# K and V pages of two neighbouring heads in one transfer of 256 rows, in half of each layer of a two-layer decode kernel

## The chip, the cores and the metric

One Trainium2 chip; the kernel runs on one of its cores. The core has a matrix engine (PE, with its weight loads shown apart as PEld), a vector engine (DVE), a scalar engine (ACT), a general engine (POOL) and a sync engine (SP) whose queue (SPq) issues the transfers. Sixteen DMA engines move the data from the chip's main memory (HBM) into the on-chip memory (SBUF, 128 partitions).

The metric is the device time of one launch in microseconds (us), the median of several runs. Beside it stands one profiled execution, whose span runs from its first to its last instruction.

## The reference

One token passes twice through the same attention block and the same gated feed-forward block (the layers are called 0 and 1 here; both read the same weights and the same caches):

```
x = x + A(layernorm(x));  x = x + B(layernorm(x));  x = x + A(layernorm(x));  x = x + B(layernorm(x))

A: q = x @ wq                                   # 640 -> 32 heads of 192
   scores = q . k[last 4096 rows] / sqrt(192)   # per head, 4096 x 192 bf16 = 1.5 MiB
   o = softmax(scores) @ v[last 4096 rows]      # per head, another 1.5 MiB
   return o @ wo                                # 6144 -> 640
B: return (silu(x @ w1) * (x @ w3)) @ w2        # 640 -> 1536 -> 640
```

The last 4096 of 32768 rows are used of each head's K and V. All of it is bf16, with one row of activations, so nearly all bytes are read for a single product. Since both layers use the same caches, a page of K that stays in SBUF need not be read a second time.

## The kernel before, in words

**Slots.** SBUF holds an `arena` of 16 slots (`NSLOT`), each 128 partitions x 6144 bf16 (12288 bytes per partition, 1536 KB), one page each. A page is one head's K or V window, a fifth of `wq`, or a piece of `wo`, `w1`, `w3`, `w2`. Slot s begins at element `s * PGW` of each partition's row of the one tile `arena`.

**Order of the loads.** Before anything is recorded, a list `loads` is made (L163 to L198), for each layer: five pages of `wq`; then for i = 0 to 37 the V page of place i-6 (`LEAD` is 6) and the K page of place i, as far as these exist; then `wo`, `w1`, `w3`, `w2`. A place g (0 to 31) is turned into a head by `head(layer, g)`: layer 0 takes the heads in blocks of eight as 24-31, 16-23, 8-15, 0-7, layer 1 as 8-15, 0-7, 16-23, 24-31.

**Retained pages.** The K pages of the 14 heads in `RETAIN` (0 to 8, 11, 14, 18, 21, 24) are kept from layer 0 for layer 1; their slots come free only in layer 1. One of them, head 24 (`STASH`), is copied by DVE out of its slot and back later (`stash`, L214); in layer 1 it takes a slot without a transfer. So the number of slots that circulate falls in the second half of layer 0, down to 3, and rises again in the first half of layer 1.

**Slots and transfers.** `refill` (L200) takes the next entry of `loads` as long as a slot is free, and records one `dma_start` on SP's queue into that slot (L210). `free` is first in, first out. `done(key)` (L225) puts a page's slot back on `free` when the last instruction that reads it has been recorded, and calls `refill`. All instructions are kept in the order in which they are recorded (`pin`), SP's included. A framework puts in the semaphore waits: a transfer waits for the last readers of its slot, a reader waits for the transfers that write what it reads, and each transfer also waits for the transfer eight before it, because the transfers share eight semaphores in turn. To tell which accesses touch each other, the framework compares their regions of the tile.

**Work on a page.** `attention` (L494) runs steps i = 0 to 37. In step i it first uses the V page of place i-6 (`v_page`, 16 matmuls, group `o_ps`), then the K page of place i (`k_page`): DVE turns the page in place in two halves (L300, `k_turn`), and PE multiplies it (12 matmuls, group `s_ps`). A retained K page was already turned in layer 0. After each fourth K page come the turn of the next K page, a softmax (`softmax_head`, L321 on), and a step later the placing of its result (`softmax_place`, L343). A block of four heads is closed by `combine` (L372). After step 37 follow `wo_proj` (group `y_ps`), a layernorm and `ffn` (groups `g_ps`, `u_ps`, and in layer 1 `f_ps`).

All matmuls have one line, L80, the helper that records them; they are told apart by their groups.

Of the kernel before, what the change touches and what calls it, by code (L numbers as in the profile page):

```python
# [15 lines left out]
P = 128  # L16
# [9 lines left out]
PGW = 6144  # L26
# [5 lines left out]
RETAIN = (0, 1, 2, 3, 4, 5, 6, 7, 8, 11, 14, 18, 21, 24)  # L32
# [4 lines left out]
MW = 2 * HB  # L37
PW = MW * (HB - 1) + 32
KSPLIT = 2


def _ap(t, p0, npart, off, dims):
    ps = t.ap[0][0]
    return bass.AP(t.tensor, t.offset + p0 * ps + off, [[ps, npart]] + [list(d) for d in dims])
# [3 lines left out]
def kernel(  # L48
# [13 lines left out]
    nc = tc.nc  # L62
    SK = A_k_cache.shape[2]
    S0 = SK - WIN
# [10 lines left out]
    def pin(ins):  # L75
        tc.keep_in_program_order(ins)
        return ins
# [60 lines left out]
    arena = arn.tile([P, NSLOT * PGW], BF16, name="arena")  # L138
# [3 lines left out]
    free = list(range(NSLOT))  # L142
    home = {}
    turned = set()
    loads = []

    wq_v = A_wq.rearrange("(p c) n -> c p n", c=NCH)
    wo_v = A_wo.rearrange("(b p e) n -> b p (e n)", b=H // HG, p=P, e=12)
    w1_v = B_w1.rearrange("(p c) n -> p (c n)", c=NCH)
    w3_v = B_w3.rearrange("(p c) n -> p (c n)", c=NCH)  # L150
    w2_v = B_w2.rearrange("(p f) n -> p (f n)", f=12)
# [3 lines left out]
    def head(layer, g):  # L155
        return HG * ORDER[layer][g // HG] + g % HG

    def wo_order(layer):
        last = ORDER[1][3]
        kept = [12 * ORDER[layer].index(last) + e for e in (9, 10, 11)]  # L160
        return [ci for ci in range(48) if ci not in kept] + kept

    for layer in range(2):  # L163
        for c in range(NCH):
            loads.append((("q", layer, c), [(0, PGW, wq_v[c])]))
        for i in range(H + LEAD):
            for kind, g, cache in (("v", i - LEAD, A_v_cache), ("k", i, A_k_cache)):
                if not 0 <= g < H:
                    continue
                h = head(layer, g)  # L170
                if kind == "k" and layer == 1 and h in RETAIN:
                    if h == STASH:
                        loads.append((("k", 1, h), []))
                    continue
                loads.append(((kind, layer, h),
                              [(0, PGW, cache[0, h, S0:SK, :].rearrange("(p t) d -> p (t d)", p=P))]))
        for w in range(6):
            parts = []
            for at, ci in enumerate(wo_order(layer)[9 * w:9 * w + 9]):
                blk, e = ORDER[layer][ci // 12], ci % 12  # L180
                if parts and parts[-1][2] == blk and parts[-1][3] + parts[-1][1] == e:
                    parts[-1][1] += 1
                else:
                    parts.append([at, 1, blk, e])
            parts = [(640 * at, 640 * n, wo_v[blk][:, 640 * e:640 * (e + n)]) for at, n, blk, e in parts]
            if w < 5:
                loads.append((("o", layer, w), parts))
            elif layer == 0:
                assert len(parts) == 1 and parts[0][1] == 1920
                loads.append((None, [(wo5[:], parts[0][2])]))  # L190
        loads.append((("fa", layer), [(0, PGW, w1_v[:, 0:PGW])]))
        loads.append((("fb", layer), [(0, PGW, w3_v[:, 0:PGW])]))
        loads.append((("fc", layer), [(0, 1536, w1_v[:, PGW:]), (1536, 1536, w3_v[:, PGW:]),
                                      (3072, 2560, w2_v[:, 0:2560])]))
        fd = [(0, 3200)] if layer == 0 else [(0, 1280), (1280, 1280), (2560, 640)]
        loads.append((("fd", layer), [(o, n, w2_v[:, 2560 + o:2560 + o + n]) for o, n in fd]))
        if layer == 0:
            loads.append((None, [(keep[:], w2_v[:, 5760:7680])]))  # L198

    def refill():  # L200
        while loads and (free or loads[0][0] is None):
            key, parts = loads.pop(0)
            if key is None:
                for dst, src in parts:
                    pin(nc.sync.dma_start(out=dst, in_=src))
                continue
            s = free.pop(0)
            home[key] = s
            for off, n, src in parts:
                pin(nc.sync.dma_start(out=arena[:, s * PGW + off:s * PGW + off + n], in_=src))  # L210
            if not parts:
                stash(arena[:, s * PGW:s * PGW + PGW], False)

    def stash(x, save):  # L214
        xu, pu, ru = x.bitcast(U32), pss[:].bitcast(U32), rest[:].bitcast(U32)
        at = 0
        for t, lo, n in [(pu, 512 * k, 512) for k in range(5)] + [(pu, MB + MN, 512 - MN), (ru, 0, MN)]:
            a, p = xu[:, at:at + n], t[:, lo:lo + n]
            pin(nc.vector.tensor_copy(out=p if save else a, in_=a if save else p))
            at += n  # L220

    def page(key):
        return arena[:, home[key] * PGW:home[key] * PGW + PGW]

    def done(key):  # L225
        free.append(home.pop(key))
        refill()
# [64 lines left out]
    def k_turn(layer, g):  # L292
# [4 lines left out]
        x = page(key)  # L297
        w = PGW // KSPLIT
        for sp in range(KSPLIT):
            pin(nc.vector.transpose(x[:, w * sp:w * (sp + 1)].bitcast(U32), x[:, w * sp:w * (sp + 1)].bitcast(U32)))  # L300
# [193 lines left out]
    def attention(layer):  # L494
# [30 lines left out]
        wo_proj(layer)  # L525

    refill()
    for layer in range(2):
        attention(layer)
# [32 lines left out]
```

## Time and profile before

| what | value |
|---|---|
| median of 3 runs | 528.83 us (528.5 to 529.74) |
| the profiled execution | 528.32 us |
| its span | 526.6 us |
| mean granted TensorE clock | 0.716 |
| PE busy | 275.0 us (52%), 2403 matmuls |
| DVE busy | 256.4 us (49%), 393 instructions |
| ACT busy | 62.5 us (12%) |
| SP's transfers | 221.59 MB, 99.3% of the 16 DMA engines' span |
| K and V pages loaded | 50 K and 64 V, median 29.2 us from issue to landing |

The busy rows are shares of the whole span. The row of the transfers is the time that packets took, as a share of the span of all 16 DMA engines together. The chain of work that ended last is followed back from the last instruction to what released it; its shares by engine add up to the span.

### The profile page before, as it was taken

The numbers are of one execution on the slowest core, as the hardware profiler recorded it, in microseconds if no ns is written. First come the engines' busy times: TensorE is split into PE (matmuls) and PEld (weight loads), VectorE is DVE, ScalarE is ACT, GpSimd is POOL, SyncE is SP. The second block draws the span as 40 slices with busy tenths as digits, with TensorE's granted clock in tenths as the row PEclk, the third lists the DMA queues.
The fourth block names the chain that finished last, engine by engine and source line by source line (L and its number), as shares of the span: only waits on it lengthen the run. The fifth ranks groups of instructions, "written<-read, shape, count | busy, mean of one in ns | idle before, by whom it ended". The sixth has DMA issues, their size and how long they took to land.

```text
span 526.6 us, 5978 instructions
## 1 busy us (share of the span) xinstructions
PE 275.0 (52%) x2403; PEld 112.6 (21%) x2403; DVE 256.4 (49%) x393; ACT 62.5 (12%) x192; POOL 16.2 (3%) x74
## 2 busy tenths in 40 slices
PE   2344644472655644455545555687254756345455
PEld 1111211131222221122112112233022322112113
DVE  1199676556657475654002139531475645753001
ACT  1002020110102020112001002022111120202000
POOL 4000000000000000000000000000000000001000
PEclk9997968666756776586556558988677886686557
DMA  8999999999999999999999999999999999999995
GB/s 349 429 430 433 426 428 427 433 432 427 427 428 432 432 426 429 428 432 423 419 431 422 427 428 427 420 431 427 428 428 431 429 428 429 429 431 428 424 432 242
DMA packets 22355, 221.97 MB, mean 421 GB/s; under 512 B 2616, under 2 KB 2744, under 8 KB 5176
## 3 DMA queue, kind: packets, MB, share of 16 engines
q1 hardware_dynamic: 22184, 221.59, 99.3%
q8 instruction: 19, 0.31, 0.2%
q14 instruction: 8, 0.07, 0.0%
q10 hardware_dynamic: 144, 0.00, 0.0%
HBM read 221.58 MB, written 0.00 MB: 421 GB/s over the span
## 4 chain that ended last, share of the span: by engine, by line
DMA 85%; PE 7%; DVE 5%; issue 1%; ACT 1%; SPq 1%; DVEq 0%; ACTq 0%
DMA arena<-in_A_k_cache_dram 51%; DMA arena<-in_A_v_cache_dram 16%; DMA arena<-in_A_wo_dram 9%; DMA arena<-in_B_w_dram 6%; DMA arena<-in_A_wq_dram 3%; DVE arena L300 3%; PE s_ps L80 3%; PE o_ps L80 2%; PE y_ps L80 1%; SPq L210 1%; PE q_ps L80 1%; PE u_ps L80 0%; PE pss L80 0%; ACT w L337 0%; DVE t L322 0%
## 5 line engine op out<-in xcount | busy, mean ns | idle before, releaser
L80 PE MATMUL s_ps<-arena,wst 128*32 128x512 bf16 x768 | 153.7, 512 | 171.3 <-DVE arena L300 84.5
L300 DVE STREAM_TRANSPOSE arena<-arena 128x1536 uint32<-128x1536 uint32 x100 | 171.2, 1754 | 75.0 <-DMA arena<-in_A_k_cache_dram 74.6
L80 PE MATMUL o_ps<-arena,ptm 128*8 128x384 bf16 (+1 forms) x1024 | 113.5, 421 | 12.9 <-DMA arena<-in_A_v_cache_dram 12.9
L80 PEld LDWEIGHTS <-wst 128*32 128x32 bf16 x768 | 53.1, 115 | 256.2 <-issue 227.1
L80 PEld LDWEIGHTS <-ptm 128*8 128x8 bf16 (+1 forms) x1024 | 40.0, 99 | 49.9 <-issue 40.3
L332 ACT ACTIVATE tb<-m 32x16 f32<-32x16 f32 x16 | 3.4, 214 | 280.4 <-DVE m L329 280.4
L350 ACT COPY ptm<-w 32x64 bf16<-32x64 bf16 x80 | 23.6, 295 | 42.5 <-PE o_ps L80 39.3
L80 PE MATMUL y_ps<-arena,otd 128*1 128x320 bf16 x180 | 16.9, 459 | 15.1 <-DMA arena<-in_A_wo_dram 15.1
L80 PE MATMUL q_ps<-arena,xs 128*32 128x512 bf16 x120 | 14.5, 624 | 17.3 <-DMA arena<-in_A_wq_dram 14.7
L383 DVE SCALAR_TENSOR_TENSOR w<-pss,rl,mask 64x192 bf16<-64x192 f32 x16 | 6.7, 417 | 32.2 <-PE pss L80 32.2
L282 POOL COPY wst<-qt_sb 32x24 bf16<-32x24 bf16 x30 | 8.4, 281 | 432.7 <-PE s_ps L80 313.8
L340 DVE STREAM_TRANSPOSE w<-w 64x512 bf16<-64x512 bf16 x16 | 11.3, 705 | 14.4 <-ACT w L337 14.4
L248 DVE CAST w<-y_ps 128x320 bf16<-128x320 f32 x3 | 1.5, 490 | 34.4 <-PE y_ps L80 34.4
L322 DVE TENSOR_REDUCE t<-s_ps 64x1 f32<-64x512 f32 x16 | 10.6, 663 | 12.2 <-PE s_ps L80 12.1
L274 DVE CAST qt_sb<-pss 32x192 bf16<-32x192 f32 x2 | 0.7, 346 | 31.2 <-PE pss L80 31.2
L350 DVE COPY ptm<-w 32x64 bf16<-32x64 bf16 x48 | 9.9, 207 | 10.8 <-PE o_ps L80 9.6
L80 PEld LDWEIGHTS <-xs 128*32 128x32 bf16 x200 | 7.2, 119 | 35.7 <-issue 26.1
L355 DVE RECIPROCAL rl<-pss 64x1 f32<-64x1 f32 x16 | 2.6, 166 | 22.2 <-PE pss L80 22.2
L80 PEld LDWEIGHTS <-otd 128*1 128x1 bf16 x192 | 6.4, 103 | 25.8 <-issue 21.7
L337 ACT ACTIVATE w<-s_ps,nbt 64x512 bf16<-64x512 f32 x16 | 10.9, 682 | 5.6 <-DVE nbt L334 5.6
L376 ACT CAST w<-o_ps 128x384 bf16<-128x384 f32 x16 | 7.7, 479 | 33.0 <-PE o_ps L80 23.7
L80 PE MATMUL pss<-w,sel 128*64 128x192 bf16 x32 | 6.3, 286 | 9.5 <-ACT w L376 6.4
(82 smaller groups left out, 111.8 us busy)
## 6 DMA issues: line engine op xcount, KB each, us to landing
arena<-in_A_v_cache_dram SPq DMA_DIRECT2D x64, 1536.0 KB, 29.2
arena<-in_A_k_cache_dram SPq DMA_DIRECT2D x50, 1536.0 KB, 29.2
arena<-in_A_wq_dram SPq DMA_DIRECT2D x10, 1536.0 KB, 9.3
arena<-in_A_wo_dram SPq DMA_DIRECT2D x6, 1440.0 KB, 15.3
arena<-in_B_w_dram SPq DMA_DIRECT2D x4, 1536.0 KB, 11.1
arena<-in_A_wo_dram SPq DMA_DIRECT2D x4, 960.0 KB, 16.8
arena<-in_A_wo_dram SPq DMA_DIRECT2D x4, 480.0 KB, 21.8
arena<-in_B_w_dram SPq DMA_DIRECT2D x4, 384.0 KB, 14.6
```

The source lines that it names most:

```text
L80: return pin(nc.tensor.matmul(*a, **k))
L210: pin(nc.sync.dma_start(out=arena[:, s * PGW + off:s * PGW + off + n], in_=src))
L282: pin((engs[a].copy if engs[a] is nc.scalar else engs[a].tensor_copy)(out=dst, in_=src))
L300: pin(nc.vector.transpose(x[:, w * sp:w * (sp + 1)].bitcast(U32), x[:, w * sp:w * (sp + 1)].bitcast(U32)))
L322: pin(nc.vector.reduce_max(out=t0[:, 0:1], in_=s_ps[0:64, :], axis=AX.X))
L332: pin(nc.scalar.mul(out=tb[32:64, :].rearrange("p (a z) -> p a z", a=4)[:, :, 0:HB], in_=mb, mul=-SCALE))
L337: pin(nc.scalar.activation(out=e[:], in_=s_ps[0:64, :], func=ACTF.Exp, bias=nbt[:, 0:1], scale=SCALE, accum_out=l[:]))
L340: pin(nc.vector.transpose(et[:], e[:]))
L350: pin((eng.copy if eng is nc.scalar else eng.tensor_copy)(out=dst, in_=src))
L355: pin(nc.vector.reciprocal(out=rl[half], in_=rl_ps[half]))
L376: pin(nc.scalar.copy(out=o_sb[:, 0:384], in_=o_ps[:, 0:384]))
L383: pin(nc.vector.scalar_tensor_tensor(out=om, in0=ot_ps[half], scalar=rl[half], in1=mask[half].unsqueeze(2).broadcast_to([64, 16, 12]), op0 ...
```

## The change

In the first 16 places of layer 0 and the last 16 places of layer 1 (`PAIRS`), the pages of places g and g+1 (g even) are loaded by one transfer, where both are to be loaded: the entry of `loads` then names two keys, stands at the place of the first, and its source is `cache[0, h:h+2, ...]` seen as 128 rows x 2 heads x 6144. In layer 1 a K pair with a retained head in it (18/19, 20/21, 24/25) is left as it was. That makes 16 pairs in layer 0 and 13 in layer 1 (8 of V, 5 of K).

`refill` now waits, in recording, until as many slots are free as the entry has keys, takes the first ones of `free`, sorts them, and records one `dma_start` whose destination is one access pattern over both slots: 128 partitions x 2 (with a step of the distance between the two slots) x 6144. Pages are used and given back one by one as before.

```diff
+PAIRS = (range(0, 16), range(16, 32))
...
                 h = head(layer, g)
+                if g in PAIRS[layer] and (kind == "v" or layer == 0 or not {h - g % 2, h - g % 2 + 1} & set(RETAIN)):
+                    if g % 2 == 0:
+                        loads.append(([(kind, layer, h), (kind, layer, h + 1)],
+                                      [(0, PGW, cache[0, h:h + 2, S0:SK, :].rearrange("h (p t) d -> p h (t d)", p=P))]))
+                    continue
...
     def refill():
-        while loads and (free or loads[0][0] is None):
-            key, parts = loads.pop(0)
-            if key is None:
+        while loads:
+            keys, parts = loads[0]
+            if keys is None:
                 for dst, src in parts:
                     pin(nc.sync.dma_start(out=dst, in_=src))
+                loads.pop(0)
                 continue
-            s = free.pop(0)
-            home[key] = s
-            for off, n, src in parts:
-                pin(nc.sync.dma_start(out=arena[:, s * PGW + off:s * PGW + off + n], in_=src))
+            n = len(keys)
+            if len(free) < n:
+                return
+            at = sorted(free.pop(0) for _ in range(n))
+            home.update(zip(keys, at))
+            loads.pop(0)
+            s = at[0]
+            for off, w, src in parts:
+                dst = arena[:, s * PGW + off:s * PGW + off + w]
+                if n > 1:
+                    dst = _ap(arena[:], 0, P, s * PGW, [[(at[1] - s) * PGW, 2], [1, PGW]])
+                pin(nc.sync.dma_start(out=dst, in_=src))
             if not parts:
                 stash(arena[:, s * PGW:s * PGW + PGW], False)
```

All other entries of `loads` are wrapped in a list of one key and load as before.

More of the change, by code (lines that the diff above doesn't have):

```diff
@@ L164 @@
         for c in range(NCH):
-            loads.append((("q", layer, c), [(0, PGW, wq_v[c])]))
+            loads.append(([("q", layer, c)], [(0, PGW, wq_v[c])]))
         for i in range(H + LEAD):
@@ L170 @@
                 h = head(layer, g)
+                if g in PAIRS[layer] and (kind == "v" or layer == 0 or not {h - g % 2, h - g % 2 + 1} & set(RETAIN)):
[3 more added lines that the diff above has]
+                    continue
                 if kind == "k" and layer == 1 and h in RETAIN:
                     if h == STASH:
-                        loads.append((("k", 1, h), []))
+                        loads.append(([("k", 1, h)], []))
                     continue
-                loads.append(((kind, layer, h),
+                loads.append(([(kind, layer, h)],
                               [(0, PGW, cache[0, h, S0:SK, :].rearrange("(p t) d -> p (t d)", p=P))]))
@@ L186 @@
             if w < 5:
-                loads.append((("o", layer, w), parts))
+                loads.append(([("o", layer, w)], parts))
             elif layer == 0:
@@ L190 @@
                 loads.append((None, [(wo5[:], parts[0][2])]))
-        loads.append((("fa", layer), [(0, PGW, w1_v[:, 0:PGW])]))
-        loads.append((("fb", layer), [(0, PGW, w3_v[:, 0:PGW])]))
-        loads.append((("fc", layer), [(0, 1536, w1_v[:, PGW:]), (1536, 1536, w3_v[:, PGW:]),
+        loads.append(([("fa", layer)], [(0, PGW, w1_v[:, 0:PGW])]))
+        loads.append(([("fb", layer)], [(0, PGW, w3_v[:, 0:PGW])]))
+        loads.append(([("fc", layer)], [(0, 1536, w1_v[:, PGW:]), (1536, 1536, w3_v[:, PGW:]),
                                       (3072, 2560, w2_v[:, 0:2560])]))
         fd = [(0, 3200)] if layer == 0 else [(0, 1280), (1280, 1280), (2560, 640)]
-        loads.append((("fd", layer), [(o, n, w2_v[:, 2560 + o:2560 + o + n]) for o, n in fd]))
+        loads.append(([("fd", layer)], [(o, n, w2_v[:, 2560 + o:2560 + o + n]) for o, n in fd]))
         if layer == 0:
```

## The prediction

> **What bounds the kernel now.** I read the page first (DMA rows, queues, chain), then SP's waits, then the stretches of PE and DVE at the places where the change acts.
>
> ```profile
> DMA  8999999999999999999999999999999999999995
> q1 hardware_dynamic: 22184, 221.59, 99.3%
> DMA 85%; PE 7%; DVE 5%; issue 1%; ACT 1%; SPq 1%; DVEq 0%; ACTq 0%
> ...
> SPq L210 <- DMA arena<-in_A_v_cache_dram: 174.7, 56, 4.0
> SPq L210 <- DMA arena<-in_A_k_cache_dram: 132.4, 40, 4.7
> SPq L210 <- PE o_ps L80: 36.0, 18, 7.3
> ```
>
> The transfers fill 99.3% of the span, so they are the bound, and at most 3.7 us (0.7% of 526.6) could be won by filling them better. SP mostly waits for a transfer eight before it: eight pages are under way, and a page lands 29.2 us after its issue. This queue is the cover for everything that DVE and PE do; they are busy for half the span and wait for pages.
>
> ```profile
> 14.18 1.47 PE L80 MATMUL q_ps<-arena,xs 128*32 128x512 bf16 x12 [2.10 <-DMA arena<-in_A_wq_dram]
> 17.83 1.47 PE L80 MATMUL q_ps<-arena,xs 128*32 128x512 bf16 x12 [2.17 <-DMA arena<-in_A_wq_dram]
> ...
> 25.77 3.44 DVE L300 STREAM_TRANSPOSE arena<-arena 128x1536 uint32<-128x1536 uint32 x2
> 29.13 4.11 DVE L219 COPY pss<-arena 128x512 uint32<-128x512 uint32 x6
> ...
> 339.45 0.68 DVE L322 TENSOR_REDUCE t<-s_ps 64x1 f32<-64x512 f32 x1 [1.61 <-PE s_ps L80]
> ...
> 342.38 0.70 DVE L340 STREAM_TRANSPOSE w<-w 64x512 bf16<-64x512 bf16 x1 [0.90 <-ACT w L337]
> ...
> 224.00 1.70 PE s_ps L80 x12
> ```
>
> Prices from these: a page passes in 3.65 us (17.83 - 14.18, the third and fourth page of wq). The first transfer is issued at 0.73 and has landed two pages before 14.18, at 6.9; less its own 3.65 that leaves 2.5 us of start and landing, which a full queue hides and an empty one pays. Turning a K page is 3.44, its product 1.70, a softmax on DVE 3.63 (339.45 to 343.08), saving the stashed page 4.3.
>
> ```profile
> 493.21 1.45 PE L80 MATMUL o_ps<-arena,ptm 128*8 128x384 bf16 x16 [2.18 <-DMA arena<-in_A_v_cache_dram]
> ...
> 515.64 1.56 PE L80 MATMUL g_ps<-arena,xs 128*32 128x384 bf16 x16 [1.31 <-DVE xs L242]
> 517.72 1.23 PE L80 MATMUL u_ps<-arena,xs 128*32 128x384 bf16 x14 [0.52 <-DMA arena<-in_B_w_dram]
> ```
>
> The last V page lands at 493.2, 33.4 us before the end; by then all other attention is done, and PE follows the weights in.
>
> **What the change removes: almost nothing.** 29 transfers fewer. SP's issues (0.33 us each) lie beside its waits. If the queue stays full, the gain is somewhere between 0 and the 3.7 us of unfilled queue; I take 0, since the page pace was already free of gaps between transfers.
>
> **What it adds: waits on pages that are not touched.** A pair's destination is one access pattern over two slots of one tile, with a step between them. The waits of the program as built show how the framework takes this. The first turn of a K page (slot 5), before and after:
>
> ```
> L300 StreamTranspose arena<-arena 128x1536 [waits DMAHW6_49]
> L315 StreamTranspose arena<-arena 128x1536 [waits DMAHW6_49,DMAHW3_49]
> ```
>
> The second wait is for the pair of V places 2 and 3, which goes to slots 0 and 15: the pair counts as touching everything from its first slot to its last. So a page that has long landed may be read only when the newest pair whose span covers its slot has landed. And that pair is the newest in SP's queue, so its landing means that the queue is empty behind it: the next transfer needs a slot that only this reading will free. Each such place costs the queue 2.5 us plus the work up to the release.
>
> Where it happens follows from `free` (first in, first out), slot by slot.
>
> Layer 0. The first K pair (5,6) waits for (0,15), the 16th and 17th page: 6.9 + 16 x 3.65 = 65.3, where the turn began at 25.77 before. The 21 pages already queued last until 6.9 + 20 x 3.65 = 79.9. The next pair needs the second page done: 65.3 + 3.44 (turn) + 4.3 (stash) + 3.44 + 1.70 = 78.2, its data begins 2.5 later: a gap of 0.8. Two pairs, issued at 78.2 and 85.1, last until 95.3; the next needs 85.1 + 3.44 + 3.63 (softmax) + 3.44 = 95.6 (DVE runs one product ahead of PE), gap 2.8. The other pairs lie in neighbouring slots or one apart, (1,2), (3,4), (7,8), (9,10), and cover nearly nothing; DVE (two turns, 6.9 us, in the 14.6 us of four pages) regains its lead. Sum 3.6 us, bounds 0 and 11 (one full gap of 8.8 + 2.5).
>
> Layer 1. Here the slots come back in scattered order. Pairs, slots, and the page that waits:
> - K 22/23 (3,13): K 16 in slot 4 waits. Turn 3.44 + softmax 3.63 + product 1.70 = 8.8 until its slot is free.
> - V 18/19 (4,15): the stashed page going back to slot 11, then K 17 in slot 9: 3.65 (six copies and one) + 3.44 + 1.70 = 8.8.
> - K 26/27 (1,12): K 20 in slot 7, again with a softmax: 8.8.
> - K 28/29 (2,10): K 22 in slot 3: 3.44 + 1.70 = 5.1.
> - K 30/31 (8,13): K 24 in slot 11, already turned: 1.7.
> - V 26/27 (4,11): K 25 in slot 9: 5.1.
>
> Work 38.3, and six starts of 2.5: 53.3 us with the queue empty. The price from the row shown for the return of the stash:
>
> ```profile
> L219 DVE COPY arena<-pss x6: 479/680/692, 381.6 to 384.6; 128x512 uint32<-128x512 uint32 x5, 128x320 uint32<-128x320 uint32 x1
> ```
>
> Bounds: with a start of 1.0 (little more than the issue) instead of 2.5 it is 44; with products at 1.91, the slowest in the chain, and a product of a V page (1.45) in front of each release, 63. I take 53, as turns and softmax, most of the sum, hardly vary (1727 to 1779 ns a half turn).
>
> The end. K 28 in slot 2 waits for the very last pair, V 30/31 in (1,5). When that lands, all the rest of the attention stands before PE: turn 3.44, softmax 3.63, placing 0.7, three turns 10.3, one combine 1.1, a product 1.7, a softmax 3.63, placing 1.5, four V pages at 1.2 and a combine 2: about 32.5. Then `wo`, 90-odd matmuls at the rate of the rows behind 496 (24 in 1.85), 8.5; layernorm up to `g_ps` 3.5; 16 matmuls 1.56; and 8.9 from the first `u_ps` (517.72) to the end. Sum 55, where it was 33.4: 21.5 later. The weights (30 us of transfers) come in beside it. Bounds 13 (V pages at 0.8, a faster granted clock) to 28.
>
> A pair also lands as one, 3.65 us late for its first page; this is hidden while the queue holds more than one pair, and already in the counts where it doesn't.
>
> Sum 3.6 + 53.3 + 21.5 = 78.4 on the profiled execution's 528.3, 606.7; the median is 0.5 above that execution, so 607.
>
> **The rivals.**
> - *Not slower.* The covering pairs land before the pages they cover are due, because the queue runs 29 us ahead; then only merged transfers remain: 528.3, at best 524.6. For it: the lead, and that layer 0's pairs are mostly neighbours. Against: in layer 1 the covering pair is recorded at the very release before the waiting read, so lead is what gets used up. It decides at one gap: if K 16's turn starts without waiting for K 22/23. Chance 0.04, with half of it for a real gain.
> - *Gaps, but no backlog at the end.* If PE keeps up better, the end is hidden beside the weights: 528.3 + 57 = 585. Chance 0.10, with anything from 540 to 588, as some gaps may be shorter too.
> - *Every pair drains.* If all 13 pairs of layer 1 empty the queue, at a mean of 53.3 / 6 = 8.9 us: 13 x 8.9 + 25 = 141, so 669. Against: (6,8), (5,14), (0,7), (3,6), (9,15) are followed by another pair before a covered read. Chance 0.08, with anything above 630.
> - *Slow rows.* Each of a pair's rows is followed by one 12.6 MB away in HBM. wq's rows lie 61 KB apart and pass at the 3.65 of contiguous pages, which speaks against an effect of distance. Were the rate halved, 58 pages would cost 58 x 3.65 = 212 more, 819. Chance 0.02. [...]
>
> **How the numbers follow.** Forecast 607, chance 0.76, within 528.8 + 57 (0 + 44 + 13) = 586 and 528.8 + 102 (11 + 63 + 28) = 631. To hold 0.8 the range reaches down to 582, into the upper part of the case without a backlog (0.04 of its 0.10); the top stays at 630. Below lies 0.10, above 0.10. A change below 0.2% (1.1 us) could not be told from none. Slower 0.96, same 0.02, faster 0.02.
>
> **What the profile after would show.** The queue's DMA row falls below 9 in layer 1's second half, in about six places (behind 410), the mean GB/s to about 368 (221.97 MB in 604). DVE's first turn starts near 65 instead of 25.8. DVE waits at L315 for V transfers, not K alone. SP's waits move from DMA to PE. Behind the last V landing lie some 55 us. Wrong would be: a DMA row full of nines, or a page pace for pairs other than 7.3.

## The result, and the profile after

The changed kernel takes 615.45 us (median of 6, 612.11 to 616.46), the kernel before 529.08 us (6, 528.5 to 529.9): 1.1627 times as long, 95% interval 1.1612 to 1.1642. The profiled execution took 615.45 us with a span of 613.7, 87.1 us more than the 526.6 before.

From the page of the changed kernel, the DMA share and rate in 40 slices, SP's transfers, and the chain by engine:

```profile
DMA  8999999999999999999999999992566459549970
GB/s 360 431 433 428 430 383 396 424 433 428 429 428 429 431 426 433 405 421 421 432 428 412 426 431 427 430 430 89 205 222 292 186 225 378 238 183 406 367 289 3
...
q1 hardware_dynamic: 21720, 221.59, 86.4%
...
DMA 56%; PE 21%; DVE 17%; issue 4%; ACT 2%; SPq 0%; POOL 0%; DVEq 0%; ACTq 0%; POOLq 0%
```

The same 221.59 MB now fill 86.4% of a longer span. A slice is 15.3 us, and up to the 27th the queue is as full as before, except for a dent at the sixth and seventh. From 414 us on it is not: there layer 1 comes to its last 16 places. PE and DVE, which held 12% of the chain, hold 38%.

The waits of SP's queue, longest first (us in total, times, longest):

```profile
SPq L225 <- DVE arena L315: 177.7, 22, 37.9
SPq L225 <- PE s_ps L81: 102.1, 33, 17.4
SPq L225 <- PE o_ps L81: 77.2, 32, 8.5
SPq L225 <- DMA arena<-in_A_v_cache_dram: 54.9, 21, 3.7
```

And those of DVE:

```profile
DVE arena L315 <- DMA arena<-in_A_k_cache_dram: 98.3, 11, 51.0
DVE arena L315 <- DMA arena<-in_A_v_cache_dram: 73.4, 4, 39.6
```

Before, SP waited for earlier transfers; now it waits for DVE and PE to give slots back. And the turn of a K page (L315) waits 73.4 us for transfers of V, which it never reads. DVE's time line shows the long waits of layer 0's first turn and of layer 1's last 16 places, for pairs of V and of K (start, length, and in brackets the idle time before and what ended it):

```profile
65.53 3.44 DVE L315 STREAM_TRANSPOSE arena<-arena 128x1536 uint32<-128x1536 uint32 x2 [39.59 <-DMA arena<-in_A_v_cache_dram]
...
419.24 3.44 DVE L315 STREAM_TRANSPOSE arena<-arena 128x1536 uint32<-128x1536 uint32 x2 [50.97 <-DMA arena<-in_A_k_cache_dram]
...
439.23 3.48 DVE L234 COPY arena<-pss 128x512 uint32<-128x512 uint32 x6 [12.92 <-DMA arena<-in_A_v_cache_dram]
...
472.93 3.44 DVE L315 STREAM_TRANSPOSE arena<-arena 128x1536 uint32<-128x1536 uint32 x2 [18.52 <-DMA arena<-in_A_k_cache_dram]
...
500.19 6.76 DVE L315 STREAM_TRANSPOSE arena<-arena 128x1536 uint32<-128x1536 uint32 x4 [12.39 <-DMA arena<-in_A_k_cache_dram]
...
537.76 3.44 DVE L315 STREAM_TRANSPOSE arena<-arena 128x1536 uint32<-128x1536 uint32 x2 [24.31 <-DMA arena<-in_A_v_cache_dram]
...
562.36 3.44 DVE L315 STREAM_TRANSPOSE arena<-arena 128x1536 uint32<-128x1536 uint32 x2 [5.07 <-DMA arena<-in_A_v_cache_dram]
```

And the issues of SP over the same stretch. The first after each wait follows the turn and the product of the page that had waited:

```profile
384.42 0.38 SPq L225 DMA_DIRECT2D arena<-in_A_k_cache_dram  x1
429.06 0.37 SPq L225 DMA_DIRECT2D arena<-in_A_v_cache_dram  x1
449.02 0.34 SPq L225 DMA_DIRECT2D arena<-in_A_k_cache_dram  x1
454.08 0.37 SPq L225 DMA_DIRECT2D arena<-in_A_v_cache_dram  x1
456.44 0.37 SPq L225 DMA_DIRECT2D arena<-in_A_k_cache_dram  x1
482.60 0.37 SPq L225 DMA_DIRECT2D arena<-in_A_v_cache_dram  x1
485.97 0.37 SPq L225 DMA_DIRECT2D arena<-in_A_k_cache_dram  x1
506.43 0.37 SPq L225 DMA_DIRECT2D arena<-in_A_v_cache_dram  x1
509.85 0.37 SPq L225 DMA_DIRECT2D arena<-in_A_k_cache_dram  x1
527.71 24.84 SPq L225 DMA_DIRECT2D arena<-in_A_v_cache_dram  x3
```

Read together: at 419.24 the pair of K places 22 and 23 has landed, and nothing is behind it: SP has issued nothing since 384.42. DVE turns the page of place 16, the softmax and the product follow, and only at 429.06 does SP have two slots for the next pair. That lands 10.2 us later, when the stash may go back (439.23). Then the same again.

### The profile page after: what moved, and what is told of

It reads as the page before. It is cut to its first block, busy times and chain, and to the rows that moved or that the text cites. A ratio compares the mean times of both kernels' runs of the same rounds, so it can differ in the third digit from the quotient of the medians.

```text
span 613.7 us, 5942 instructions
## 1 busy us (share of the span) xinstructions
PE 267.1 (44%) x2403; PEld 114.9 (19%) x2403; DVE 255.1 (42%) x393; ACT 62.5 (10%) x192; POOL 16.1 (3%) x74
## 3 DMA queue, kind: packets, MB, share of 16 engines
q1 hardware_dynamic: 21720, 221.59, 86.4%
## 4 chain that ended last, share of the span: by engine, by line
DMA 56%; PE 21%; DVE 17%; issue 4%; ACT 2%; SPq 0%; POOL 0%; DVEq 0%; ACTq 0%; POOLq 0%
DMA arena<-in_A_k_cache_dram 32%; DMA arena<-in_A_v_cache_dram 14%; PE s_ps L81 13%; DVE arena L315 12%; DMA arena<-in_A_wq_dram 6%; PE o_ps L81 4%; DMA arena<-in_A_wo_dram 3%; DMA arena<-in_B_w_dram 2%; PE y_ps L81 1%; PE pss L81 1%; ACT w L352 1%; PE u_ps L81 1%; DVE pss L234 1%; DVE t L337 1%; DVE arena L234 1%
## 5 line engine op out<-in xcount | busy, mean ns | idle before, releaser
L315 DVE STREAM_TRANSPOSE arena<-arena 128x1536 uint32<-128x1536 uint32 x100 | 170.0, 1749 | 172.1 <-DMA arena<-in_A_k_cache_dram 98.3
L81 PEld LDWEIGHTS <-wst 128*32 128x32 bf16 x768 | 55.7, 119 | 363.8 <-issue 323.6
L81 PE MATMUL o_ps<-arena,ptm 128*8 128x384 bf16 (+1 forms) x1024 | 115.5, 424 | 5.3 <-DMA arena<-in_A_v_cache_dram 5.3
L81 PE MATMUL y_ps<-arena,otd 128*1 128x320 bf16 x180 | 11.9, 379 | 8.0 <-DMA arena<-in_A_wo_dram 8.0
L365 DVE COPY ptm<-w 32x64 bf16<-32x64 bf16 x48 | 9.9, 207 | 10.2 <-PE o_ps L81 9.1
L391 ACT CAST w<-o_ps 128x384 bf16<-128x384 f32 x16 | 7.7, 479 | 44.5 <-DVE ptm L365 27.7
L297 ACT COPY wst<-qt_sb 32x24 bf16<-32x24 bf16 x30 | 8.8, 292 | 2.8 <-DVE qt_sb L289 2.2
## 6 DMA issues: line engine op xcount, KB each, us to landing
arena<-in_B_w_dram SPq DMA_DIRECT2D x4, 1536.0 KB, 11.8
```

The costliest lines, as they stand in the source:

```text
L81: return pin(nc.tensor.matmul(*a, **k))
L297: pin((engs[a].copy if engs[a] is nc.scalar else engs[a].tensor_copy)(out=dst, in_=src))
L365: pin((eng.copy if eng is nc.scalar else eng.tensor_copy)(out=dst, in_=src))
L391: pin(nc.scalar.copy(out=o_sb[:, 0:384], in_=o_ps[:, 0:384]))
```

## The experiments

The comparisons below are medians; "before" is the kernel before on the same chip. Three theories were held against each other: SPAN, that readers wait for pairs whose first and last slot lie around their page; TWO SLOTS, that taking two slots at once starves the queue; BIG TRANSFER, that a transfer of 256 rows is dear in itself.

**Two transfers per pair.** Same order of loads and same slots as the changed kernel, but no pattern over two slots:

```diff
                 dst = arena[:, s * PGW + off:s * PGW + off + w]
+                if n > 1 and True:
+                    for t in range(2):
+                        pin(nc.sync.dma_start(out=arena[:, at[t] * PGW:at[t] * PGW + PGW],
+                                              in_=src[:, t, :]))
+                    continue
```

> As the changed kernel (same order of loads, same two slots taken at once), but each pair is issued as two transfers of 128 rows, one per slot. Theory SPAN (a reader waits for any pair whose first and last slot lie around its page): no access pattern covers a foreign slot, so 528 to 531 us, no empty stretch of the queue. Theory TWO SLOTS (taking two slots at once and the changed order of the loads empty the queue): 612 to 617. Theory BIG TRANSFER (a transfer of 256 rows is itself dear, 87 us / 29 = 3.0 us each): 528 to 531.

528.55 us against 528.67, ratio 0.9995 (0.9986 to 1.0005). TWO SLOTS falls: the order and the waiting for two slots cost nothing.

**Merged where the slots are neighbours.** The lines above, under `if n > 1 and at[1] - at[0] > 1`.

> As the changed kernel, but a pair is issued as one transfer only if its two slots are neighbours; otherwise as two of 128 rows. 13 pairs stay merged, 16 are split. SPAN: a pair in neighbouring slots covers no foreign slot, 528 to 531 us. TWO SLOTS: 612 to 617. BIG TRANSFER: 529 + 13 x 3.0 = 568.

528.68 us, ratio 1.0004 (0.9994 to 1.0013). Thirteen merged transfers (7 of K, 6 of V), no loss.

**All 29 pairs merged, all in neighbouring slots.**

```diff
-            at = sorted(free.pop(0) for _ in range(n))
+            lone = [x for x in free if x ^ 1 not in free]
+            both = [x for x in free if x & 1 == 0 and x + 1 in free]
+            if n == 1:
+                at = [(lone or free)[0]]
+            elif both:
+                at = [both[0], both[0] + 1]
+            elif len(free) < 99:
+                return
...
+            for x in at:
+                free.remove(x)
```

> All 29 pairs merged, but slots are given out so that each pair gets two neighbouring ones: a single page prefers a slot whose neighbour is taken, a pair waits until two neighbours are free. SPAN: 528 to 534 us (a pair may wait a little longer for its slots; the first turn starts near 26 again). BIG TRANSFER and TWO SLOTS: 612 or more.

528.79 us, ratio 1.0002 (0.9993 to 1.0012). From its view of the DMA queues, SP's transfers and the issues of V and K (count, KB each, median us from issue to landing):

```profile
q1 hardware_dynamic: 21720, 221.59, 99.2%
...
arena<-in_A_v_cache_dram SPq DMA_DIRECT2D x16, 3072.0 KB, 44.4
arena<-in_A_v_cache_dram SPq DMA_DIRECT2D x32, 1536.0 KB, 19.5
arena<-in_A_k_cache_dram SPq DMA_DIRECT2D x13, 3072.0 KB, 37.8
```

And the first turn on DVE's time line:

```profile
29.01 3.44 DVE L330 STREAM_TRANSPOSE arena<-arena 128x1536 uint32<-128x1536 uint32 x2 [3.05 <-DMA arena<-in_A_k_cache_dram]
```

The 29 transfers of 3 MB are all there, with the rows of two heads in turn, and the queue is 99.2% full. BIG TRANSFER falls, and with it the thought that rows 12.6 MB apart are slow. The pairs of V now take 44.4 us from issue to landing and the single pages of V 19.5, where every page took 29.2 before. At 3.65 us a page, 44.4 us are about 12 pages under way instead of 8, which neither costs nor earns anything. The first turn starts at 29.0 instead of 65.5; the 3 us against 25.8 before are the wait for a pair of K that lands as one.

**The spans kept, the transfers made small.** Each pair as two transfers that write the left and the right half of the columns of both slots:

```diff
                 if n > 1:
-                    dst = _ap(arena[:], 0, P, s * PGW, [[(at[1] - s) * PGW, 2], [1, PGW]])
+                    for o in (0, PGW // 2):
+                        dst = _ap(arena[:], 0, P, s * PGW + o, [[(at[1] - s) * PGW, 2], [1, PGW // 2]])
+                        pin(nc.sync.dma_start(out=dst, in_=src[:, :, o:o + PGW // 2]))
+                    continue
```

> As the changed kernel, but each pair is issued as two transfers that write the first and then the second half of the columns of both slots: 256 rows of 6144 bytes, 1.5 MB each, so no transfer is larger than before, and the access patterns still reach over the same slots. SPAN: the same empty stretches, 612 to 620 us. BIG TRANSFER: 528 to 532, as no transfer has more bytes than before (or 3.0 us for each of 58 if rows in turn from two heads are the dear thing: 700).

616.7 us against 528.67, ratio 1.1649 (1.1625 to 1.1674). Its DMA row is nearly that of the changed kernel:

```profile
DMA  8999999999999999999999999992556459649960
```

With no transfer larger than before, the whole loss is back. The spans of the patterns are enough for it, and with the third experiment nothing else of the change is needed. One rival is left by these four runs: that writing into two slots far apart is slow in itself. The changed kernel's trace speaks against it. The pair for slots 4 and 15, alone in the queue, was there 10.17 us after its issue (429.06 to 439.23), which is two pages of 3.65 and 2.9 for the start. And all packets of SP's queue together took 86.4% of 613.7 us, 530 us, against 523 before: 7 us more at most, not 87.

**One layer at a time.** `PAIRS = (range(0, 16), range(0, 0))`, and the other way round:

> Pairs in layer 0 alone (16 of 29). SPAN: only the wait of the first turn for the pair in slots 0 and 15, a gain or loss that the changed kernel's trace puts at 3.2 us: 531 to 534 us. BIG TRANSFER: 529 + 16 x 3.0 = 577.

532.24 us against 528.57, ratio 1.0068 (1.005 to 1.0086): 3.7 us.

> Pairs in layer 1 alone (13 of 29). SPAN: nearly all of the loss, 66 us in the queue and 18 at the end in the changed kernel; the slots come round in another order without layer 0's pairs, so some spans are shorter: 598 to 616 us. BIG TRANSFER: 529 + 13 x 3.0 = 568.

603.45 us, ratio 1.1414 (1.1373 to 1.1454): 74.9 us. The two losses add up to 78.6, not to 86.4: without the pairs of layer 0 the slots come free in another order (by `free`, the pair of K places 16 and 17 gets slots 6 and 11 instead of 4 and 9), and other spans come about. So the loss depends on the order in which slots happen to come free.

**One pair alone.** First the last one (V of places 30 and 31 of layer 1), then a wide one in the middle (K of places 22 and 23):

```diff
-                if g in PAIRS[layer] and (kind == "v" or ...):
+                if layer == 1 and kind == "v" and g >= 30:
```

> One pair alone: the V pages of places 30 and 31 of layer 1, the last pair. SPAN: its slots reach over K pages that are still to be turned, so the rest of the attention stands behind its landing: no empty queue, but the end comes later by about the 18 us of the changed kernel, 543 to 552 us. Rival ONE GAP EACH (every pair costs the same, 87 / 29 = 3.0 us): 532.

548.22 us, ratio 1.0357 (1.0331 to 1.0382): 19.7 us for one transfer fewer. On DVE's time line:

```profile
493.54 3.44 DVE L315 STREAM_TRANSPOSE arena<-arena 128x1536 uint32<-128x1536 uint32 x2 [47.75 <-DMA arena<-in_A_v_cache_dram]
```

DVE idles 47.75 us in front of a page that is long there. Up to the landing the queue has no break. From 493.5 to the end it is 53.0 us, against 33.4 behind the last V landing before, so the whole loss is the work that stands behind this pair.

> One pair alone: the K pages of places 22 and 23 of layer 1, with a wide span. SPAN: the page of place 16 waits for it; the queue runs empty once or twice, at most one gap of 11 us, and is full again afterwards, so the loss is carried to the end: 535 to 542 us. Rival ONE GAP EACH: 532. Rival ABSORBED (the compute regains it before the end): 529.

540.78 us, ratio 1.0228 (1.0212 to 1.0245): 12.2 us, within the range. The turn of place 16 waits for the pair, and two issues of SP come late:

```profile
412.96 3.44 DVE L315 STREAM_TRANSPOSE arena<-arena 128x1536 uint32<-128x1536 uint32 x2 [47.60 <-DMA arena<-in_A_k_cache_dram]
...
424.05 0.33 SPq L225 DMA_DIRECT2D arena<-in_A_v_cache_dram  x1
432.55 0.33 SPq L225 DMA_DIRECT2D arena<-in_A_k_cache_dram  x1
```

By the DMA rate in slices of 1 us, the queue falls short of its usual 428 GB/s by 7.0 us of transfers in front of the page issued at 424.05 and by 4.8 around the next issue, together 11.8 of the 12.2. ABSORBED and ONE GAP EACH fall: the queue is full again afterwards, but this loss was not regained.

**Do the losses add up?** The changed kernel without its last pair:

> The changed kernel without its last pair (V of places 30 and 31 of layer 1 as two single transfers). If the losses add up, it gives back what the last pair costs alone, 19.6 us: 596. By the waits of the changed kernel's trace it gives back only the 5.07 us that DVE idles for that pair before the turn of place 28, since the pair before it still holds the turn of place 27 back: 609 to 612.

609.31 us, ratio 1.1534 (1.1508 to 1.156): 6.1 us less than the changed kernel, within the 609 to 612 that the waits had given, and not 19.7. So the losses don't add up. The pair before it (V of places 28 and 29) still holds back the turn of place 27, at 548.97 on DVE's time line:

```profile
541.05 3.42 DVE L315 STREAM_TRANSPOSE arena<-arena 128x1536 uint32<-128x1536 uint32 x2
548.97 6.76 DVE L315 STREAM_TRANSPOSE arena<-arena 128x1536 uint32<-128x1536 uint32 x4 [4.50 <-DMA arena<-in_A_v_cache_dram]
```

But the turn of place 28 now follows it without a break (6.76 for four halves), which gives back the 5.07 us of idling that the changed kernel shows at 562.36. The six runs lie 6.4 us apart (606.28 to 612.63), so the last us of the 6.1 is not explained.

**The price of a product.** The next section needs it: a product cost 2.6 us in the gaps, where I had 1.70. To see whether this is the price of a low clock after idling, thirty extra matmuls, whose result is not used, keep PE busy before two of them:

```diff
                         k_turn(layer, i + 1)
+                        if layer == 1 and i + 1 in (16, 20):
+                            y = page(k_source(layer, i + 1)[0])
+                            for _ in range(30):
+                                mm(m_ps[0:32, 0:192], lhsT=wst[:, 0, 0, :], rhs=y[:, 0:192], start=True, stop=True)
```

> The changed kernel with 30 extra matmuls (192 columns, into unused columns of pss, their result is not used) before the products of places 16 and 20 of layer 1; they wait for the first half turn of that page, so that PE works in the 5 us in which it idles now before the product. If the idle time before it sets the granted clock at 0.5 and so the price of a product of 2.6 us, those two products take 1.5 to 1.9 us, their gaps shrink by about 1 us each, and the time by about 2, 613 to 614. Rival (the product is slow for another reason): products still at 2.6 us, 615 to 617.

611.29 us, ratio 1.1557 (1.1537 to 1.1576), below the interval of the changed kernel (1.1612 to 1.1642); the medians differ by 4.2 us. PE's time line at the second place:

```profile
472.81 4.64 PE L81 MATMUL pss<-arena,wst 128*32 128x192 bf16 x28 [16.58 <-DVE arena L315]
...
478.57 1.19 PE L81 MATMUL s_ps<-arena,wst 128*32 128x512 bf16 x8
...
480.59 1.63 PE L81 MATMUL s_ps<-arena,wst 128*32 128x512 bf16 x12
```

This product begins at 478.57 and lets SP issue at 480.26, 1.7 us later, where it was 2.8 (479.83 to 482.60). Its row of 8 takes 1.19, where in the changed kernel (479.83) it takes 1.89 at a clock of 0.50. At the first place with the matmuls it is 1.9 us to the issue (427.06 to 428.91). The mean granted clock was 0.77 from 474 to 484 and 0.65 from 421 to 430, where the changed kernel has 0.50 over stretches that lie alike about the product (475.26 to 485.26 and 420.23 to 429.23). If it went once from 0.50 to 1.00, the values of the changed kernel at 424 to 426 and 455 to 456.4, it rose at about 478.6 and 427.3; by this estimate the two products ran at 1.00 and 0.93. So the product became cheaper where the clock was higher, as expected.

How much of the 4.2 us comes from this is not shown. The extra matmuls also delay the product: from the start of the turn to the issue it is 9.4 us (419.47 to 428.91) and 9.3 (470.98 to 480.26), where it was 9.8 and 9.7, so each place gains 0.4. The rest of the lead in this trace lies elsewhere, and a trace without added matmuls has it too. The run without the last pair is the same program up to that pair, and there SP comes to the pair of V places 26 and 27 as early. The issue in the changed kernel, with the matmuls, and without the last pair:

```profile
527.71 24.84 SPq L225 DMA_DIRECT2D arena<-in_A_v_cache_dram  x3
...
524.02 24.88 SPq L225 DMA_DIRECT2D arena<-in_A_v_cache_dram  x3
...
523.02 24.59 SPq L225 DMA_DIRECT2D arena<-in_A_v_cache_dram  x4
```

Executions of the same instructions thus differ by more than the matmuls were to earn.

## Why the prediction was right, and where its sum was off

The forecast of 607 (582 to 630) held at 615.45, and for its reason; two of its terms were mis-sized, in opposite directions.

*Nothing gained by fewer transfers*: right. Merged without spans, all 29 give a ratio of 1.0002.

*Waits for pages that are not touched*: right. The span alone (halves) brings the loss; without it (split, neighbours) there is none. The framework's rule was read from one pair of wait lists, and the runs bear it out.

*Layer 0, 3.6 us*: 3.7 with its pairs alone; first turn forecast at 65.3, found at 65.53. The sum agrees better than its parts. In that run the transfers, by their rate, fall short by 1.8 us around 80 and by 1.4 around 96, where the forecast had gaps of 0.8 and 2.8; that the two misses cancel is luck.

*Layer 1's queue, 53.3 us*: right in its places, too small in its sum, and its bound of 63 did not hold. All six are there, in the forecast order. Of the 87.1 us, the end takes 17.9 (below) and layer 0 3.7, which leaves 65.5. (Counted as transfers missing at 428 GB/s between 414 and 562 us, it is 66.) Work first, from a landing to the next issue, forecast and found: 8.8 and 9.8 (419.24 to 429.06), 8.8 and 9.8 (439.23 to 449.02), 8.8 and 9.7 (472.93 to 482.60), 5.1 and 6.2 (500.19 to 506.43), 1.7 and 2.8 (524.93 to 527.71), 5.1 and 6.2 (537.76 to 544.00): 44.5 instead of 38.3. Each is one us too short, and the product is that one us. The stretches of the products in the changed kernel, and three of the kernel before (start and end, length, busy time of PE, PEld, DVE, ACT, POOL, then the granted clock, the DMA share and GB/s):

```profile
426.29:428.89 2.60, 2.60 (x22) 1.04 (x24) 0.02 (x1) 0.00 (x0) 0.00 (x0) 0.50 0.00 0
...
524.93:527.69 2.76, 2.76 (x22) 1.12 (x24) 0.00 (x0) 0.00 (x0) 0.00 (x0) 0.50 0.00 0
541.25:543.97 2.72, 2.72 (x12) 0.85 (x12) 0.60 (x3) 0.48 (x1) 0.00 (x0) 0.50 0.00 0
```

```profile
337.89:339.42 1.53, 1.53 (x22) 0.76 (x25) 0.00 (x0) 0.00 (x0) 0.00 (x0) 1.00 1.02 434
219.98:222.58 2.60, 2.60 (x22) 1.05 (x24) 2.20 (x3) 0.00 (x0) 0.00 (x0) 0.50 0.98 414
224.00:225.70 1.70, 1.70 (x14) 0.68 (x10) 0.48 (x3) 1.38 (x5) 0.00 (x0) 0.83 0.95 405
```

The row I took (224.00) belongs to a product that came right behind other work, at a clock of 0.83. Four microseconds earlier the same kernel had shown the price that I needed: 2.60 at 0.50, for a product after PE had idled for 6.69 us. The 1.91 of the forecast's upper bound was no better: the chain shows slower products in several pieces, so 1.91 was only the slowest in one piece. All six products behind the gaps ran at 0.50 (2.57 to 2.76 us). The traces show this clock behind idling: PE had idled 41.25 us before the product at 426.29 and 6.69 before the one at 219.98, both at 0.50, and with PE kept busy for 4.6 us (472.81) the product that followed was down to 1.7, at 1.00 by the estimate above. After how much idling the clock falls, and how much work brings it back, is not shown.

The start of an empty queue, forecast 2.5, was 2.9 (a pair issued at 429.06 was there at 439.23, 10.17 less two pages of 3.65): six of them, 17 instead of 15. With 44.5 that is 62 of the 65.5. The rest is in places that I had not counted, by the DMA rate. The single page of place 25 is alone in the queue, as the next issue follows after 5.06 us (449.02 to 454.08) and a page takes 3.65: 1.5. The last pair is issued too late to join the one before it: 0.8. And before a wait ends the rate has already fallen off (197 and 25 GB/s in the two us from 417 to 419), which can make up what is left.

*The end, 21.5 us*: 17.9. From the last V landing to the end it is 613.7 - 562.4 = 51.3, against 33.4 before; I had 55. The V pages, four of them at 1.2 in my sum, took about 1.0 (chain of the changed kernel: 64 matmuls in 4.07, at a mean granted clock of 0.67), and `wo` behind them was faster still:

```profile
591.85 4.07 PE o_ps L81 x64
...
596.85 3.82 PE y_ps L81 x98
```

98 matmuls of `wo` take 3.82, 39 ns each, at a granted clock of 1.00. I had 8.5 from a row of 24 in 1.85, 77 ns each; between such rows PE waited for transfers of `wo` (1.06 to 2.72 us each from 498 to 511), and the clock in that row (496.62 to 498.47 in the kernel before) was 0.50. At 77 ns, 98 are 7.6, so the 8.5 was also summed too high. These two items are 5.4 below the forecast; the others, with a product of 2.6 at 0.50 among them (569.26), came out 1.7 above it.

So the clock was misjudged on both sides, for the products behind the gaps (0.50 instead of 0.83) and for `wo` at the end (1.00 instead of 0.50). The product in an idle engine was 6 us too low, starts and uncounted stretches 6 us, and the end 3.6 too high: 78.4 became 87.1.

*The rivals.* Not slower: it decided at place 16, which waited (419.24). No backlog at the end: 17.9 us of it. Every pair drains: no, the five pairs that are followed by another pair before a covered read left no gap of their own in the time line, apart from the 0.8 above. Slow rows: excluded by the 29 merged pairs at 528.79. The halved rate in this rival's 819 was my assumption, and no run shows it: with the rows of two heads in turn, the queue of that run was 99.2% full in the 526.5 us of its span, as with single pages (99.3% of 526.6).

*The signs.* DVE waited at L315 for transfers of V (73.4), as forecast. Mean rate 362 GB/s (368 forecast). SP's waits went from transfers to DVE first (177.7) and PE second, where I had named PE alone.

What stays open: how much the thirty matmuls earn, and why executions of one program differ by some us.

## What to carry to other kernels

An access pattern with a large step was, for the framework of this kernel, a write to everything in between (616.7 us with the spans, 528.79 with all pairs in neighbouring slots): after any change of a pattern's shape, look at what the readers wait for, not only at the transfer. With slots handed out first in, first out, two free slots need not be neighbours (16 of the 29 pairs here had none); with pairs in neighbouring slots, or one transfer per slot, the order cost nothing here (ratios 1.0002 and 0.9995). The full queue of this kernel gained nothing from fewer transfers, and hid nearly all of a wait of 39.6 us (layer 0 lost 3.7). Where it was emptied in layer 1, the six emptyings account for 62 of the 65.5 us lost there: 44.5 of work, with products of 2.57 to 2.76 us at a clock of 0.50, and 17 for the starts, 2.9 each by the pair issued at 429.06.

## What was not expected of the hardware

A product (11 or 12 matmuls of 512 columns in the windows above) took 1.53 us at a granted clock of 1.00, 1.70 at 0.83 and 2.60 to 2.76 at 0.50, and the changed kernel paid such a price, 2.57 to 2.76, after each of the six waits that emptied its queue. `wo`, 98 matmuls, took half as long per matmul in the changed kernel (39 ns, at a clock of 1.00) as in a row of the kernel before (77 ns, at 0.50), although nothing of it was changed.

About twelve pages under way instead of eight (44.4 us from issue to landing instead of 29.2, at 3.65 us a page) moved no faster, 99.2% against 99.3% of the span.
